# Expert sums added by a DMA from GpSimd's queue, a matrix inverse planned sooner, and ten stores moved to SyncE's queue

## The chip, the core and the metric

The kernel runs on one core of one Trainium2 chip. The metric is device time of one execution in microseconds (us); lower is better. The engines are named as in the profile: PE (TensorE, matmuls), PEld (its weight loads), DVE (VectorE), ACT (ScalarE), POOL (GpSimd), SP (SyncE, which here only issues DMAs). Each engine works through its own queue in order. DMAs are issued on the queues of SP, POOL and, at the start, ACT. A change of this kernel's time under about 0.2% (3 us) cannot be told from none.

## What is computed

A delta-rule attention feeds two expert layers:

```python
for t in range(S):                       # 768 steps, per batch (4) and head (8), D = 48
    y[:, :, t] = einsum('bhd,bhde->bhe', q[:, :, t], state)
    v_old = einsum('bhde,bhd->bhe', state, kt)
    state = state + bt * einsum('bhd,bhe->bhde', kt, vt - v_old)
x = y as (3072 tokens, 384)
for e in range(4):                       # experts: 384 -> 1024 -> 384
    out += p[:, e:e + 1] * (maximum(x @ w1[e], 0) @ w2[e])
gate = 1 / (1 + exp(-(out @ w_gate)));  return (gate * (out @ w_val)) @ w_out   # 384 -> 1536 -> 384
```

All is float32; each large matmul is done as three passes over split operands (high and low parts).

## The kernel before

**Tiling.** The sequence is cut into 12 steps of 64 positions; a step holds 256 tokens. Two steps make a pair of 512 tokens, and there are six pairs. For each pair PE runs four expert phases ("m1", 8 units each, `emit_a` and `emit_b`) and one gated phase ("m2", 12 units). In `emit_a` PE writes `ph` (line 759), ACT and DVE split it into `hhi` and `hlo`, and two units later `emit_b` sums into `acc` (line 796). A granule of weights comes in as `raw` (line 182, SP's queue, three buffers), and ACT and DVE split it into `ws`.

**Experts' sums.** At the end of an expert phase `finish` runs for the three row blocks d = 0, 1, 2. Expert 0 writes `ACC` directly. For the others DVE writes `ctmp`, the product of `acc` with the gate probabilities `pe`; then for experts 1 and 2 POOL adds it to `ACC` (line 837), and for expert 3 DVE adds it and ACT and DVE split the sum into `xhi` and `xlo` for m2. In the first pair the phases are cut differently: there two sets of three adds work on 256 columns.

**Attention.** Step c needs `XT`, the inverse of a triangular 64 x 64 matrix per head. `plan_g` makes `L` and `P` of a step (tile `LP`): the keys `KQ` are loaded on SP's queue, ACT copies them to `bdG` (lines 318 and 319), PE multiplies (`pg`, line 325), DVE scales. `l_out`, `l_off` and `p_out` then store them in DRAM (`ld`, lines 411 and 412; `pd`, line 428): five DMAs for a step from the fourth on. Once a pair is stored, `plan_inv` reads it back (`Lpp`), and DVE alone works out the inverse in 63 steps of two instructions each (`itmp`, then `Xpp`). `x_out` stores the result (`xd`, line 505, POOL's queue, two DMAs) and `x_in` reads it back in another layout (`XT`, line 508, POOL's queue). Then PE multiplies `pu` (line 357), and so on through the step's chain. `scale_v` (line 539) is two POOL multiplications of `V`, which DVE needs for `R`.

**Decode.** In the first 300 us the second layer's weights come in a packed form: ACT (`dec_scale`, lines 229 and 230), DVE and POOL (lines 239 and 240) unpack them, and POOL's queue stores them (`w_d`, line 252). They go round a few buffers, so a new ACT step waits until an older store has landed.

**Order.** The program is written out by a planner at build time. `plan(t, ...)` puts a task at a model time t of PE; `back` holds two lists, "dec" and "inv", of single DVE instructions with due times, and `fill` emits one when it is due and the model's DVE is at most 2.8 us ahead of PE. At `first` (14 or 8 us before a pair's chain) what is left of the inverse is emitted at once. `q[0]` is the queue on which stores and read-backs are issued; it is POOL's after the start.

Of the kernel before, what the change touches and what calls it, by code (L numbers as in the profile page):

```python
# [14 lines left out]
ALU = mybir.AluOpType  # L15
# [5 lines left out]
NE, FF1, FF2 = 4, 1024, 1536  # L21
# [20 lines left out]
CH1, CH2, TR1, TR2 = 78.0, 50.0, 44.0, 16.0  # L42
# [40 lines left out]
def moe_delta_kernel(  # L83
# [14 lines left out]
    nc = tc.nc  # L98
# [181 lines left out]
    q = [nc.sync, None, None]  # L280
# [109 lines left out]
    def l_out(c):  # L390
        lt = Lts[c % 2]
        r, c2 = INV_OF[c]
        steps, small = INV[r]
        l_done.add(c)
        lv = [lt[o : o + HC].rearrange("p i h t -> p (i h) t") for o in range(0, P, HC)]
        if small:
            if c2 == 0:
                ld_t[r] = dr.tile([len(steps), 2, 2, H, 2, HC, HC], F32, tag=f"ls{len(steps)}", name="ls")
                od_t[r] = dr.tile([len(steps), 2, H, 2, HC, HC], F32, tag=f"lo{len(steps)}", name="lo")
            for a in range(2):  # L400
                for bp in range(2):
                    q[0].dma_start(
                        out=ld_t[r][c2, a, :, :, bp].rearrange("i h s t -> s (i h) t"),
                        in_=lv[2 * bp + a][:, :, a * HC : (a + 1) * HC],
                    )
            return
        if c2 == 0:
            ld_t[r] = dr.tile([len(steps), 2, H, 2, HC, 3 * HC], F32, tag="ld", name="ld")
        for bp in range(2):
            ld = ld_t[r][c2, :, :, bp]  # L410
            q[0].dma_start(out=ld[:, :, :, 0:C].rearrange("i h s t -> s (i h) t"), in_=lv[2 * bp])  # L411
            q[0].dma_start(
                out=ld[:, :, :, C:].rearrange("i h s t -> s (i h) t"), in_=lv[2 * bp + 1][:, :, HC:]
            )

    def l_off(c):
        lt = Lts[c % 2]
        r, c2 = INV_OF[c]
        if INV[r][1]:
            for bp in range(2):  # L420
                q[0].dma_start(
                    out=od_t[r][c2, :, :, bp].rearrange("i h s t -> s (i h) t"),
                    in_=lt[bp * C : bp * C + HC].rearrange("p i h t -> p (i h) t")[:, :, HC:],
                )

    def p_out(c):
        pd_t[c] = dr.tile([P, 2 * H * C], F32, tag=f"pd{c % 2}", name="pd")
        q[0].dma_start(out=pd_t[c], in_=Pts[c % 2].rearrange("p i h t -> p (i h t)"))
# [375 lines left out]
    def finish(n, d):  # L804
        kind, b, e, s0, ns = PHASES[n]
        cols, w = slice(s0 * STEP, (s0 + ns) * STEP), ns * STEP
        if kind == "m2":
            o = (2 * b + s0) * STEP
            t = tp.tile([P, 2 * STEP], F32, tag="tmp", name="otmp")
            nc.scalar.copy(out=t[:, :w], in_=acc_t[d][:, :w])  # L810
            nc.sync.dma_start(out=out[d, :, o : o + w], in_=t[:, :w])
            return
        pe = p_t[n][:, :w]
        if e == NE - 1 and d == 0:
            x_hi[b, 2] = xp.tile([P, KT, 2 * STEP], F32R, tag="xhi", name="xhi")
            x_lo[b, 2] = xp.tile([P, KT, 2 * STEP], F32R, tag="xlo", name="xlo")
        new = [s for s in range(s0, s0 + ns) if (b, s, d) not in begun]
        begun.update((b, s, d) for s in new)
        for s in new:
            at = slice((s - s0) * STEP, (s - s0 + 1) * STEP)  # L820
            if len(new) == 2:
                at = slice(0, 2 * STEP)
            vec.tensor_tensor(
                out=ACC[:, d, cols][:, at], in0=acc_t[d][:, at], in1=pe[:, at], op=ALU.mult
            )
            if len(new) == 2:
                return
        if len(new) == ns:
            return
        if new:  # L830
            s1 = 1 - new[0]
            cols, w = slice(s1 * STEP, (s1 + 1) * STEP), STEP
            pe = pe[:, cols]
        a, ps = ACC[:, d, cols], acc_t[d][:, cols if new else slice(0, w)]
        t = gp.tile([P, 2 * STEP], F32, tag=("gv", "sg")[d % 2], name="ctmp")[:, :w]
        vec.tensor_tensor(out=t, in0=ps, in1=pe, op=ALU.mult)
        (nc.vector if e == NE - 1 else nc.gpsimd).tensor_tensor(out=a, in0=a, in1=t, op=ALU.add)  # L837
        if e == NE - 1:
            xh = x_hi[b, 2][:, d, cols]
            nc.scalar.copy(out=xh, in_=a)  # L840
            vec.tensor_tensor(
                out=x_lo[b, 2][:, d, cols], in0=a, in1=xh.bitcast(F32), op=ALU.subtract
            )
# [5 lines left out]
    W, M2 = {}, {}  # L849
# [8 lines left out]
    def plan(t, fn, kind=""):  # L858
        todo.append((t, len(todo), kind, fn))
# [86 lines left out]
    def plan_g(c, t):  # L946
        plan(t, lambda: load_kq(c))
        for i in range(2):
            plan(t + 12, lambda i=i: fill_bd(KQi, i))

        def g_task(i, hg):
            pg = g_bd(i, hg, KQi)
            g_l(pg, c, i, hg)
            g_p(pg, c, i, hg)

        for i in range(2):
            plan(t + 14 + 5 * i, lambda i=i: [g_task(i, hg) for hg in range(2)], "pe")
        plan(t + 23, lambda: (l_out(c), l_off(c), p_out(c)))

    class Turns:  # L960
        def __init__(self, *queues):
# [130 lines left out]
    with tc.manual_schedule():  # L1092
        pre_lo = xp.tile([P, KT, 2 * STEP], F32R, tag="xlo", name="pre_lo")
        dec_tiles()
        dpt, k2 = startup()
        q[1] = nc.sync
        vec_at[0] = 0.0
        plan(0.0, lambda: (gate_probs(dpt), load_p(0)))
        for i in range(2):
            plan(0.0, lambda i=i: s_task(0, i), "pe")  # L1100
        plan(0.0, lambda: load_ys(1))
        plan(11.0, lambda: nc.gpsimd.memset(bdG, 0.0))
        back["dec"].append((0.2, "dve", lambda: nc.scalar.square(out=k2, in_=k2)))
        back["dec"].append((1.0, "dve", lambda: norm_sum(k2, 2, 2)))
        back["dec"].append((1.5, "dve", lambda: norms(2, 4)))
        for c in (2, 3):
            back["dec"].append((2.0 + c, "dve", lambda c=c: (scale_l(c), l_out(c), l_off(c))))
        for c in (2, 3):
            back["dec"].append((4.0 + c, "dve", lambda c=c: (scale_p(c), p_out(c))))
        plan_chain(1, 1.0, 1.9)  # L1110
        plan_tr(1, 12.0, 1.0)
        plan_inv(1, *INV2)
        plan_decode(DEC0, DEC1)
        for k in range(1, NPAIR):
            w = W[k]
            if k > 1:
                r0 = max(M2[0] + 40.0, w - 270.0)
                plan_inv(k, r0, r0 + 22.0, w - CH1 - 14.0)
            if k + 1 < NPAIR:
                g0 = w - (161.0 if k > 1 else 116.0)  # L1120
                plan_norms(2 * k + 2, g0 - 8.0)
                plan_g(2 * k + 2, g0)
                plan_g(2 * k + 3, g0 + 26.0)
            plan_chain(2 * k, w - (CH1 if k > 1 else 84.0), 5.9)
            plan_chain(2 * k + 1, w - (CH2 if k > 1 else 46.0), 5.9)
            plan_tr(2 * k, w - (TR1 if k > 1 else 22.0), 4.0)
            plan_tr(2 * k + 1, w - (TR2 if k > 1 else 8.0), 4.0)
        todo.sort(key=lambda r: (r[0], r[1]))

        T, base = 0.0, 0  # L1130
        for n, (kind, b, e, s0, ns) in enumerate(PHASES):
            nf = NF1 if kind == "m1" else NF2
            part = unit_us(kind, ns) / (2 if kind == "m1" else 3)
            h = {}
            if kind == "m1":
                need = [(2 * b + s0 + s, i) for s in range(ns) for i in range(2)]
                while not all(q in x_done for q in need):
                    todo.pop(0)[3]()
            for u in range(nf):
                now[0] = T = T + part * (1 if kind == "m1" else 2)  # L1140
                h[u] = emit_a(n, base, u)
                slot()
                if u == 1 and n + 1 < len(PHASES):
                    load_p(n + 1)
                if LAG <= u < nf - 1:
                    now[0] = T = T + part
                    emit_b(n, base, [u - LAG], [h.pop(u - LAG)])
                    slot()
            now[0] = T = T + part * (LAG + 1)
            us = sorted(h)  # L1150
            emit_b(n, base, us, [h[u] for u in us])
            slot()
            base += NG1 if kind == "m1" else NG2
# [74 lines left out]
```

## Time and profile before

| | |
|---|---|
| median of 3 runs | 1490.71 us (1489.71 to 1491.36) |
| the profiled execution | 1488.77 us, of which 1487.1 us are its span |
| PE | 1430.0 us busy, 96% of the span |
| DVE | 1051.8 us, 71% |
| ACT | 585.0 us, 39% |
| POOL | 271.3 us, 18% |
| chain that ended last | PE 65%, by lines 759 (34%) and 796 (26%); DVE 2%, DMA 1% |

PE is busy nearly throughout. Read the 40 slices of 37 us first: they show where PE is not at nine tenths and where the granted clock falls. Then read PE's waits, each of which names the engine or the DMA that ended it, and the timeline around the longest of them. The clock of PE has two levels, 1.2 and 2.4 GHz; the profile gives it as a share of full speed.

### The profile page before, as it was taken

The page shows a single profiled execution, that of the slowest core. Times are in us where ns is not written, and L with a number is a line of the kernel's source. Part 1 is how long each engine was busy: PE and PEld are TensorE (multiplying, and loading weights), DVE is VectorE, ACT ScalarE, POOL GpSimd, SP SyncE. Part 2 cuts the span into 40 slices and gives each one's busy share as a digit, 9 for nine tenths or more (in the row PEclk, how much of TensorE's full clock was granted, in tenths as well). Part 3 has the DMA queues.
Part 4 walks back from the last instruction along what each step waited for, and adds up shares of the span by engine and source line. Part 5 has one row for each costly group of instructions (what it writes and reads, how often), then busy time and mean ns, then how long its engine had stood idle before and what let it go on. Part 6 is the DMA issues. An engine that isn't in the chain of part 4 may idle for free.

```text
span 1487.1 us, 24739 instructions
## 1 busy us (share of the span) xinstructions
PE 1430.0 (96%) x9703; PEld 1188.9 (80%) x9703; DVE 1051.8 (71%) x1805; ACT 585.0 (39%) x953; POOL 271.3 (18%) x318
## 2 busy tenths in 40 slices
PE   6899998999999799999999999999999999999999
PEld 5687876887877688888888888888888888888787
DVE  6579997847899577788667888667888655444553
ACT  4335554525433244343344343244433343333343
POOL 3165465710012200012200001310001210001000
PEclk7889999999999899999999999999999999999999
DMA  9485796695453855554684445585333553433231
GB/s 226 109 269 188 237 293 221 192 241 152 145 133 117 208 151 135 158 155 126 173 204 142 138 137 164 154 213 158 125 103 103 141 155 96 134 103 103 85 96 64
DMA packets 95668, 232.21 MB, mean 156 GB/s; under 512 B 24800, under 2 KB 28320, under 8 KB 93520
## 3 DMA queue, kind: packets, MB, share of 16 engines
q1 hardware_dynamic: 79760, 186.65, 42.5%
q0 software_dynamic: 11376, 42.54, 10.8%
q10 hardware_dynamic: 4416, 1.44, 0.4%
q8 instruction: 76, 1.25, 0.4%
q14 instruction: 40, 0.33, 0.1%
HBM read 199.74 MB, written 26.92 MB: 152 GB/s over the span
## 4 chain that ended last, share of the span: by engine, by line
PE 65%; DVE 2%; DMA 1%; issue 1%; ACT 0%; POOL 0%; DVEq 0%; ACTq 0%
PE ph L759 34%; PE acc L796 26%; PE pu L357 1%; PE pg L325 1%; PE pk L549 1%; PE yt L582 1%; PE ps L620 1%; PE yt L583 1%; DMA XT<-xd 0%; DMA xd<-Xpp 0%; DVE Xpp L110 0%; DVE itmp L110 0%; DVE ws L110 0%; DVE hlo L110 0%; DVE ctmp L110 0%
## 5 line engine op out<-in xcount | busy, mean ns | idle before, releaser
L759 PE MATMUL ph<-xhi,ws 128*128 128x512 f32 (+1 forms) x2064 | 632.2, 388 | 1.3 <-ACT xhi L840 0.8
L796 PE MATMUL acc<-hhi,ws 128*128 128x512 f32 (+1 forms) x1632 | 496.5, 386 | 1.9 <-ACT hhi L775 0.9
L759 PEld LDWEIGHTS ph<-xhi,ws 128*128 128x128 f32 x2064 | 381.8, 189 | 78.9 <-ACT xhi L840 1.2
L759 PE MATMUL ph<-xlo,ws 128*128 128x512 f32 (+1 forms) x1032 | 398.1, 386 | 0.3 <-DVE xlo L110 0.3
L796 PEld LDWEIGHTS acc<-hhi,ws 128*128 128x128 f32 x1632 | 304.5, 190 | 62.4 <-ACT hhi L766 1.6
L110 DVE TENSOR_TENSOR ws<-raw,ws 128x768 fp32r<-128x768 f32 x308 | 300.8, 980 | 46.1 <-ACT ws L190 42.8
L796 PE MATMUL acc<-hlo,ws 128*128 128x512 f32 (+1 forms) x816 | 315.1, 386 | 11.3 <-DVE hlo L110 11.3
L190 ACT CAST ws<-raw 128x768 fp32r<-128x768 f32 x308 | 252.6, 829 | 65.7 <-PE acc L796 60.1
L766 ACT ACTIVATE hhi<-ph 128x512 fp32r<-128x512 f32 (+1 forms) x200 | 116.2, 581 | 410.0 <-PE ph L759 407.1
L759 PEld LDWEIGHTS ph<-xlo,ws 128*128 128x128 f32 x1032 | 194.4, 188 | 41.0 <-DVE xlo L110 1.9
L110 DVE SCALAR_TENSOR_TENSOR hlo<-ph,hhi 128x512 fp32r<-128x512 f32 (+1 forms) x200 | 132.9, 666 | 116.7 <-ACT hhi L766 116.6
L796 PEld LDWEIGHTS acc<-hlo,ws 128*128 128x128 f32 x816 | 154.8, 190 | 44.8 <-DVE hlo L110 14.5
L110 DVE TENSOR_TENSOR itmp<-Xpp,Lpp 128x62 f32<-128x62 f32 (+29 forms) x344 | 165.8, 489 | 12.2 <-DMA Lpp<-ls 7.4
L110 DVE TENSOR_TENSOR Xpp<-Xpp,itmp 128x62 f32<-128x62 f32 (+29 forms) x344 | 165.3, 488 | 6.6
L110 DVE TENSOR_TENSOR gv<-ph,sg 128x512 f32<-128x512 f32 x72 | 49.7, 690 | 105.6 <-PE ph L759 92.7
L837 POOL TENSOR_TENSOR ACC<-ACC,ctmp 128x512 f32<-128x512 f32 (+1 forms) x39 | 50.9, 1313 | 345.1 <-DVE ctmp L110 344.7
L775 ACT CAST hhi<-gv 128x512 fp32r<-128x512 f32 x72 | 44.7, 621 | 160.6 <-DVE gv L110 160.6
L110 DVE TENSOR_TENSOR hlo<-gv,hhi 128x512 fp32r<-128x512 f32 x72 | 51.1, 710 | 49.4 <-ACT hhi L775 49.4
L411 POOL DMA_DIRECT2D ld<-LP x16 | 10.7, 670 | 352.8 <-DVE LP L110 352.8
L773 ACT ACTIVATE sg<-ph 128x512 f32<-128x512 f32 x72 | 43.0, 597 | 69.0 <-PE ph L759 68.9
L110 DVE TENSOR_TENSOR ctmp<-acc,pe 128x512 f32<-128x512 f32 (+1 forms) x57 | 37.5, 659 | 23.2 <-PE acc L796 23.1
L357 PEld LDWEIGHTS pu<-R,XT 64*64 64x64 f32 x1024 | 33.0, 140 | 14.5 <-issue 10.6
(169 smaller groups left out, 1042.5 us busy)
## 6 DMA issues: line engine op xcount, KB each, us to landing
raw<-in_wp SPq DMA_DIRECT2D x200, 384.0 KB, 3.1
raw<-w_d SPq DMA_DIRECT2D x108, 384.0 KB, 3.6
KQ<-in_kq SPq DMA_DIRECT2D x9, 896.0 KB, 7.5
Lpp<-ld POOLq DMA_DIRECT2D x8, 768.0 KB, 14.7
pe<-p_d SPq DMA_DIRECT2D x23, 256.0 KB, 4.2
dec_a<-in_wp SPq DMA_DIRECT2D x15, 384.0 KB, 5.2
Lpp<-in_wp SPq DMA_DIRECT2D x14, 384.0 KB, 4.6
pd<-LP POOLq DMA_DIRECT2D x10, 512.0 KB, 4.9
```

The source lines that it names most:

```text
L110: return fn(*args, **kw)
L190: nc.scalar.copy(out=w[:, 0], in_=t)
L325: nc.tensor.matmul(out=pg[:, j], lhsT=bdG[:, i, h], rhs=kq_t[i][0:112, :, h], start=True, stop=True)
L357: nc.tensor.matmul(out=out[o : o + C], lhsT=lhsT[o : o + C], rhs=rhs[o : o + C], start=True, stop=True)
L549: nc.tensor.matmul(out=pk[0:C, h], lhsT=KS[C:112, i, h], rhs=rhsA[C:112, i, h], start=True, stop=True)
L582: nc.tensor.matmul(out=dst[:, 0], lhsT=fa[:, cols], rhs=YQ[0:112, 0, i, h], start=True, stop=True)
L759: nc.tensor.matmul(out=res[q], lhsT=lt, rhs=rt, start=(k == 0 and j == 0), stop=(k == KT - 1 and j == 2))
L766: nc.scalar.activation(out=hh, in_=res[0], func=AF.Relu)
L773: nc.scalar.activation(out=sg, in_=res[0], func=AF.Sigmoid)
L775: nc.scalar.copy(out=hh, in_=gv)
L796: nc.tensor.matmul(out=acc_t[d][:, :w], lhsT=lt, rhs=rt, start=(u == 0 and j == 0), stop=(u == nf - 1 and j == 2),)
L837: (nc.vector if e == NE - 1 else nc.gpsimd).tensor_tensor(out=a, in0=a, in1=t, op=ALU.add)
```

## The change

Three things are edited. In `finish` the POOL addition for experts 1 and 2 becomes a DMA on POOL's queue that adds `ctmp` to `ACC` in SBUF (39 instructions in all). In `plan_g` the stores of `L` and `P` are put 1 us later and, for steps 4 and 5, issued on SP's queue (`l_off` has nothing to do for these steps and is no longer called). In the planner's loop the read of the inverse for pairs 2 to 5 is due 2 us sooner, its first DVE step 7 us sooner and its last 6 us sooner.

```diff
         vec.tensor_tensor(out=t, in0=ps, in1=pe, op=ALU.mult)
-        (nc.vector if e == NE - 1 else nc.gpsimd).tensor_tensor(out=a, in0=a, in1=t, op=ALU.add)
-        if e == NE - 1:
+        if e < NE - 1:
+            nc.gpsimd.dma_start(out=a, in_=t, accum_op=ALU.add)
+        else:
+            nc.vector.tensor_tensor(out=a, in0=a, in1=t, op=ALU.add)
             xh = x_hi[b, 2][:, d, cols]
...
-        plan(t + 23, lambda: (l_out(c), l_off(c), p_out(c)))
+        def leave():
+            q[0] = nc.sync if c < 6 else nc.gpsimd
+            l_out(c)
+            p_out(c)
+            q[0] = nc.gpsimd
+
+        plan(t + 24, leave)
...
-                r0 = max(M2[0] + 40.0, w - 270.0)
-                plan_inv(k, r0, r0 + 22.0, w - CH1 - 14.0)
+                r0 = max(M2[0] + 38.0, w - 270.0)
+                plan_inv(k, r0, r0 + 17.0, w - CH1 - 20.0)
```

PE's and ACT's queues keep their order. On DVE the steps of the inverses move against the rest. At the start of the inverse of steps 4 and 5 (`itmp 128x63` is its first instruction) DVE's queue changes like this, - before and + now:

```order
 L110 TENSOR_TENSOR hlo<-gv,hhi 128x512
 L110 TENSOR_TENSOR ws<-raw,ws 128x768
-L110 TENSOR_TENSOR gv<-ph,sg 128x512
-L110 TENSOR_TENSOR hlo<-gv,hhi 128x512
-L110 TENSOR_TENSOR ws<-raw,ws 128x768 x2
 L110 TENSOR_TENSOR itmp<-Xpp,Lpp 128x63
 L110 TENSOR_TENSOR Xpp<-Xpp,itmp 128x63
```

The first step now stands four instructions sooner; `gv`, `hlo` and `ws` follow a few steps later.

At the end of the same inverse (its last instruction is `Xpp<-Xpp,itmp 128x32`, three rows below these) the last splits of weights and hidden values ahead of it move down:

```order
 L110 TENSOR_TENSOR Xpp<-Xpp,itmp 128x30x4
 L110 TENSOR_TENSOR itmp<-Xpp,Lpp 128x93
+L110 TENSOR_TENSOR ws<-raw,ws 128x768
+L110 SCALAR_TENSOR_TENSOR hlo<-ph,hhi 128x512
 L110 TENSOR_TENSOR Xpp<-Xpp,itmp 128x31x3
 L110 TENSOR_TENSOR itmp<-Xpp,Lpp 128x62
```

The pair comes from above: before, it stood behind `itmp 128x252`, twelve instructions higher. What stands ahead of the inverse's last instruction, taken together, is the same as before.

On POOL's queue, in the decode, the five stores of step 4 go (those of step 5, thirty instructions later, go likewise):

```order
 L240 TENSOR_TENSOR Xpp<-Xpp,dec_a 128x384
 L252 DMA w_d<-dec_b 128x384
-L411 DMA ld<-LP_117 32x16x64
-L412 DMA ld<-LP_117 32x16x32
-L411 DMA ld<-LP_117 32x16x64
-L412 DMA ld<-LP_117 32x16x32
-L428 DMA pd<-LP_117 128x1024
 L539 TENSOR_TENSOR V<-V,nrm_all 128x384 x2
 L239 TENSOR_TENSOR dec_b<-dec_b 128x384
```

On SP's queue they now stand between a weight load and the load of `KQ` for the next step:

```order
 L225 DMA Lpp<-in_wp 128x768
 L182 DMA raw<-in_wp 128x768
+L411 DMA ld<-LP_117 32x16x64
+L412 DMA ld<-LP_117 32x16x32
+L411 DMA ld<-LP_117 32x16x64
+L412 DMA ld<-LP_117 32x16x32
+L428 DMA pd<-LP_117 128x1024
 L283 DMA KQ<-in_kq 112x2048
 L182 DMA raw<-in_wp 128x768
```

SP waits there for DVE to have written `LP`. Besides, on POOL's queue the two `xd` stores of the inverse of steps 4 and 5 now stand ahead of `scale_v`, where they stood behind it.

## Rows read from the trace of the kernel before

**Rows 1.** The page's part 2: PE's granted clock in 40 equal slices, in tenths.
```profile
PEclk7889999999999899999999999999999999999999
```
**Rows 2.** PE's waits: line waited for, us in total, times, longest.
```profile
PE acc L796 <- DVE hlo L110: 11.3, 7, 2.3
```
**Rows 3.** Timeline of PE: start, us, instruction, xcount, [idle before, what ended it].
```profile
243.21 1.01 PE L325 MATMUL pg<-KQ,bdG 112*128 112x128 f32 x3 [5.70 <-ACT bdG L319]
...
492.88 0.62 PE L796 MATMUL acc<-hhi,ws 128*128 128x512 f32 x2
...
506.65 0.41 PE L357 MATMUL pu<-R,XT 64*64 64x48 f32 x2 [7.49 <-DMA XT<-xd]
508.20 3.65 PE L357 MATMUL pu<-R,XT 64*64 64x48 f32 x62 [1.14 <-DMA XT<-xd]
```
**Rows 4.** Busy time by stretch: PE, PEld, DVE, ACT, POOL, clock, DMA share, GB/s.
```profile
240.00:260.00 20.00, 15.54 (x122) 13.21 (x123) 14.20 (x26) 10.06 (x18) 5.80 (x8) 0.83 0.54 174
342.30:481.20 138.90, 134.40 (x618) 110.29 (x617) 124.43 (x213) 52.90 (x82) 16.97 (x18) 1.00 0.48 138
500.00:520.00 20.00, 12.21 (x150) 10.55 (x151) 6.05 (x9) 3.90 (x7) 8.03 (x11) 0.74 1.00 225
```
**Rows 5.** The chain that ended last, in order of time: start, us, what.
```profile
517.72 7.70 PE ph L759 x33
...
733.15 6.12 PE acc L796 x27
...
747.10 7.71 PE ph L759 x33
```
**Rows 6.** Timeline of DVE.
```profile
346.21 0.22 DVE L110 TENSOR_TENSOR itmp<-Xpp,Lpp 128x63 f32<-128x63 f32 x1
...
464.68 0.58 DVE L110 TENSOR_TENSOR itmp<-Xpp,Lpp 128x408 f32<-128x408 f32 x1
465.29 1.55 DVE L110 TENSOR_TENSOR Xpp<-Xpp,itmp 128x408 f32<-128x408 f32 x1
...
481.17 0.68 DVE L110 SCALAR_TENSOR_TENSOR hlo<-ph,hhi 128x512 fp32r<-128x512 f32 x1
...
486.26 0.26 DVE L110 TENSOR_TENSOR Xpp<-Xpp,itmp 128x93 f32<-128x93 f32 x1
...
487.31 0.22 DVE L110 TENSOR_TENSOR Xpp<-Xpp,itmp 128x32 f32<-128x32 f32 x1
```
**Rows 7.** Timeline of ACT.
```profile
235.69 0.55 ACT L229 ACTIVATE Xpp<-dec_a 128x384 f32<-128x384 f32 x1 [5.06 <-DMA w_d<-Xpp]
...
478.62 0.60 ACT L766 ACTIVATE hhi<-ph 128x512 fp32r<-128x512 f32 x1 [2.76 <-PE ph L759]
```
**Rows 8.** Timeline of POOL in the decode.
```profile
223.71 0.69 POOL L411 DMA_DIRECT2D ld<-LP  x1
...
226.95 1.75 POOL L539 TENSOR_TENSOR V<-V,nrm_all 128x384 f32<-128x384 f32 x2
...
231.25 0.61 POOL L252 DMA_DIRECT2D w_d<-Xpp  x1
```
**Rows 9.** Timelines of DVE and of SP's queue around the stores of step 4.
```profile
216.75 0.41 DVE L110 TENSOR_TENSOR LP<-pg,mask_sb 128x256 f32<-128x256 f32 x1
...
215.69 0.40 SPq L283 DMA_DIRECT2D KQ<-in_kq  x1
220.82 0.33 SPq L182 DMA_DIRECT2D raw<-in_wp  x1
```
**Rows 10.** Busy time by stretch of 4 us in the decode, columns as above.
```profile
200.00:204.00 4.00, 2.80 (x19) 2.25 (x18) 3.90 (x7) 3.68 (x7) 3.08 (x3) 1.00 1.04 412
...
228.00:232.00 4.00, 4.00 (x20) 3.27 (x19) 3.96 (x7) 1.01 (x2) 3.90 (x5) 1.00 1.03 357
```
**Rows 11.** POOL's adds as a group (xcount, busy, mean ns, idle before), and a DMA group.
```profile
L837 POOL TENSOR_TENSOR ACC<-ACC,ctmp 128x512 f32<-128x512 f32 (+1 forms) x39 | 50.9, 1313 | 345.1 <-DVE ctmp L110 344.7
...
YQ<-pd POOLq DMA_DIRECT2D x20, 256.0 KB, 5.2
```

## The prediction

> **What bounds the kernel now.** PE is busy for 96% of the span, so only its idle time and its half-clock time can be won. I read the slices of the granted clock first [rows 1]: after the start-up the clock is at nine tenths or full except in one slice, the 14th (483 to 520 us). Then PE's waits [rows 2]: the waits for `hlo` come to 11.3 us in seven pieces, none over 2.3. Two others are longer, and the timeline of PE gives them [rows 3]: 5.70 us ending at 243.21, put down to ACT's `bdG`, and 7.49 + 1.14 = 8.63 us ending at 506.65 and 508.20, put down to the read-back of `XT`. The stretches around them show the third loss, the clock [rows 4]: it is 0.83 in 240 to 260 and 0.74 in 500 to 520, against 1.00 in 342 to 481. PE had stood idle just before each fall to the lower of its two levels. What the second place costs in all comes from the chain [rows 5]: from 492.88 [rows 3] to the 33 matmuls of `ph` at 517.72 are 24.84 us, while the same pass later, from the `acc` group at 733.15 to `ph` at 747.10, takes 13.95. The loss is 10.89 us, of which 8.63 are waiting and 2.26 the clock. For the first place: 20 us at 0.83 lack 3.4 us of clock; half of the 3.2 us in which PE still stood there cost nothing, which leaves 1.8. So the two places hold 5.7 + 1.8 + 8.6 + 2.3 = 18.4 us, and that is all I see that this change can reach.
>
> **The change, part by part.** *The inverse, sooner.* DVE ends the inverse of steps 4 and 5 at 487.31 + 0.22 = 487.53, and `XT` ends PE's wait at 506.65 [rows 3, 6]. Between stand only the issue of `xd` on POOL, two stores and two read-backs, so each us that DVE ends sooner is one less of the 8.63. DVE's queue is in order and the same work stands ahead of the last row as before; a start four instructions sooner than 346.21 [rows 6] alone gives nothing. What gives is idle time: DVE is busy 124.43 of the 138.90 us from 342.3 to 481.2 [rows 4], so 14.5 us are idle there, in which it stood at a matmul result or a weight load while inverse steps, which need neither, were queued behind. With the inverse steps due sooner these fill the gaps, and the splits come just in time. How far this goes is bounded by the last split that still stands ahead of the end: that `hlo` waits for ACT's `hhi`, which ends at 478.62 + 0.60 = 479.22 [rows 7]; then the `hlo` takes 0.68 and the rest of the inverse 1.27 (from 486.26 to 487.53) [rows 6]. So the end is 481.17 at the soonest, 6.4 us earlier. Of these 6.4, some 1.9 come from the POOL additions (below), and 4.5 must come out of the 14.5 idle us. I take the full 6.4, since less than a third of the idle time does it. The low end is 1.9, if no gap is filled. The rest of the wait at `XT` is then 8.6 - 6.4 = 2.2 us. Some `hlo` now stand behind a few inverse steps of 0.2 to 0.6 us [rows 6], which makes PE wait about 1 us before it comes to `XT`. That costs nothing as long as it stays below the rest of 2.2, which it shortens. With so short a rest I count the 2.3 us of clock as won; the other end is zero, since after a wait of up to 2.3 [rows 2] nothing here says which way the clock goes. `scale_v`, now behind `xd`, takes 1.75 us for its two instructions [rows 8]; what reads `V` stands ahead of the use of `XT`, which still comes some 19 us after the inverse. Sum: 6.4 + 2.3 = 8.7 us won. The later inverses move likewise, but in [rows 2, 3] no wait of PE hangs on them.
>
> *The stores on SP's queue.* POOL issues the five stores of step 4 from 223.71 until it goes on to `V` at 226.95 [rows 8], 3.24 us. Behind them stand the scaling of `V`, an unpacking step and, at 231.25, the store `w_d` from `Xpp`. ACT's next unpacking step writes into that buffer, begins at 235.69 and has waited 5.06 us for this store [rows 7]. ACT's copies to `bdG`, for which PE waits until 243.21, are queued behind. If POOL starts that store 3.2 us sooner, ACT goes on 3.2 us sooner and so does PE: 5.7 becomes 2.5. Of the 1.8 us of clock I take half, 0.9, since a rest is left; together 4.1. The bounds are zero, if the store lands no sooner for being issued sooner, and all of 5.7 + 1.8 = 7.5, if the path behind also gets shorter. On SP the five stores wait for `LP`, ready at 216.75 + 0.41 = 217.16. Queued behind them are the load of `KQ`, issued at 215.69 before, and a weight load at 220.82 [rows 9]. Five issues at 0.33 to 0.40 us end at about 219.2, so the weight load isn't late, and `KQ` goes out about 3.5 us later, long before the `bdG` that needs it (after 235). The cover of the weight load is 1.6 us; what exceeds it lands on the splits of weights. That the stores go out some 7 us earlier than 223.71 moves their bytes into another full stretch, but no more bytes.
>
> *The additions.* A POOL addition takes 1.31 us, 39 of them 50.9 us [rows 11]. POOL is not a bound, so their removal is worth only what it gives others: a DVE step of the inverse beside one takes 1.55 us where one of the same size takes 0.58 [rows 6]. That is 0.97 us, twice in the inverse of steps 4 and 5, and these 1.9 are in the sum above. What comes instead is a DMA of 256 KB (128 in the first pair) on POOL's queue, with an issue of about 0.6 us, like the DMA issues of [rows 8], so POOL is not later. The landing has no row. The nearest is `YQ<-pd`, also 256 KB on this queue, at 5.2 us [rows 11]; with two operands read I put it between that and 15. Its reader, the next `finish`, comes a phase later, and 30 phases in 1487 us make 50 us each. So outside the decode it is hidden: zero. In the decode the DMAs are full: the share is 1.04 in 200 to 204, just where three additions run (POOL 3.08, x3), and 1.03 in 228 to 232 [rows 10]. There the new bytes push others back. One set of 3 x 256 KB at 412 GB/s [rows 10] is 1.9 us, the two sets of 3 x 128 KB are 0.95 each, 3.8 in all if each byte is moved once and 11.4 if both operands are read and the sum is written. The loads that they push back are issued ahead of their use, and none of PE's two long waits of now is put down to one, so I take zero as the likeliest and 11.4 as the end.
>
> The sum is 8.7 + 4.1 = 12.8 us. The profiled execution took 1488.8, so 1476.0; the median of the runs lies 1.9 above it, which gives 1478.
>
> **Rivals.** *Only the inverse counts.* At 228 to 232 the DMA share is 1.03 [rows 10]: the store for which ACT waits would not land sooner, however soon POOL issues it, since the same bytes are ahead of it. Against it: POOL issues it at 231.25 and ACT starts 4.4 us later, less than the 5.2 of a 256-KB transfer, so no long queue stood ahead. Result: 8.7 alone, 1482. The Trainium skill, page "Trainium Kernel Development and Optimization", section "Key Constraints", speaks for this rival: DMAs from SP's, ACT's and POOL's queues share the same 16 DMA engines, and issuing from several saves only the sequencers' issue time. By that rule the move frees 3.24 us of POOL's issue time and no transfer time; the rows on the full DMA agree, and whether the issue time was on the path no run here has yet shown.
>
> *Only the stores count.* The gaps of DVE can lie where the queue isn't rearranged enough, for instance ahead of the first step; then DVE's end moves by the 1.9 of the additions or not at all. Result: 4.1, or 4.1 + 1.9, hence 1485 to 1486.5. Against it: the splits moved down at the end of the inverse by twelve instructions, which the change shows.
>
> *All goes.* Both waits vanish with their clock: 18.4 us, 1472. It needs the path after POOL's stores and the transfers of `xd` and `XT` to shorten too; the DMA share of 1.00 in 500 to 520 [rows 4] leaves little room.
>
> *Slower.* The accumulates crowd the full queues of the decode. Weight loads and unpacked stores come late, and PE waits for `ws`. The price is up to 11.4 us of transfer, and each of three such waits may take a fall of the clock with it, 1.8 us as at 243: 16.8. With nothing won by the stores and the 8.7 kept, that is 8.1 slower, 1499. It turns slower from about 11.7 us of added waits (8.7 and the 3 that can be told). For it speaks the share of 1.04 exactly at a set; against it, that three times the bytes and no slack at all are needed.
>
> **How the numbers follow.** A change under 0.2%, 3 us, can't be told from none. The forecast, 1478, gets 0.44; only the inverse, 1482, 0.22; only the stores, about 1485.7, 0.12; all goes, 1472, 0.10; slower, 1499, 0.07; nothing, 1490, 0.05. Faster by over 0.2%, below 1487.7: the first four, less 0.02 for the upper end of the stores alone: 0.86. Within 0.2%: 0.08, from "nothing" and that 0.02 and one of the slower case's 7 hundredths, where its price stays near the turning point. Slower: 0.06. For the range I leave out the slower case and nothing, 0.12. The rest reaches from 1472 to 1486.5; two more below, about the distance between the profiled execution and the median, and a half above make 1470 to 1487.
>
> **What would show it.** For the inverse: its last DVE step ending near 481, and PE's wait for `XT` of 2 to 3 us in place of 8.6, with the clock of 500 to 520 near 1.00. For the stores: the wait at `bdG` near 2.5 us, with POOL's store from `Xpp` near 228 and ACT's step behind it near 232.5. For the additions: no DVE step of the inverse beside a POOL operation at 1.5 us, and no wait of PE at the next `finish`. The forecast is wrong if the last step ends later than 485, if new PE waits for `ws` or `raw` stand in 140 to 240, or if longer `hlo` waits in 342 to 481 exceed 2.2 us.

## The result and the profile after

| | before | after |
|---|---|---|
| median of 4 runs each | 1490.78 us | 1477.64 us (1475.94 to 1477.94) |
| ratio, with 95% interval | | 0.9913 [0.9898, 0.9928] |
| profiled execution, of which span | 1488.77, 1487.1 us | 1475.94, 1474.2 us |
| PE busy | 1430.0 us, 96% | 1426.0 us, 97% |
| POOL busy | 271.3 us | 246.1 us |

The forecast was 1478, a gain of 12.8 us on the profiled execution. The two profiled executions differ by 12.8 us. The sum agrees. But inside it errors of both signs cancel, as the experiments show, and that is luck.

The page's slices of the granted clock and PE's waits for `hlo`, after (compare [rows 1, 2]):

```profile
PEclk7889999999999999999999999999999999999999
...
PE acc L796 <- DVE hlo L110: 9.1, 6, 2.4
```

The 8 of the 14th slice is gone. The timeline of PE at the places of [rows 3], with two rows ahead of `XT` (start, us, instruction, xcount, [idle before, what ended it]):

```profile
202.74 3.02 PE L325 MATMUL pg<-KQ,bdG 112*128 112x128 f32 x16 [3.55 <-issue]
...
241.64 2.05 PE L325 MATMUL pg<-KQ,bdG 112*128 112x128 f32 x16 [2.41 <-ACT bdG L319]
...
344.30 0.73 PE L796 MATMUL acc<-hhi,ws 128*128 128x512 f32 x2 [0.52 <-DVE ws L110]
348.29 0.73 PE L796 MATMUL acc<-hhi,ws 128*128 128x512 f32 x2 [1.66 <-ACT hhi L775]
...
496.29 2.07 PE L357 MATMUL pu<-R,XT 64*64 64x48 f32 x64
```

Where after has the two waits of 0.52 and 1.66 us, before had one:

```profile
350.22 0.73 PE L796 MATMUL acc<-hhi,ws 128*128 128x512 f32 x2 [0.95 <-ACT hhi L775]
```

At `bdG` 2.41 us are left of 5.70. At `XT` nothing is left of 8.63: the 64 `pu` matmuls run without a wait. The stretches of [rows 4] (us, PE, PEld, DVE, ACT, POOL busy, clock, DMA share, GB/s) show that the clock does not fall there in this execution:

```profile
240.00:260.00 20.00, 16.78 (x148) 13.98 (x150) 17.14 (x31) 9.77 (x16) 8.49 (x10) 1.00 0.65 195
...
500.00:520.00 20.00, 19.46 (x196) 16.02 (x195) 11.73 (x20) 10.84 (x17) 3.05 (x5) 1.00 1.00 230
```

The end of the inverse of steps 4 and 5 on DVE, with the `hhi` on ACT that the last `hlo` waits for (compare [rows 6, 7]):

```profile
475.81 0.60 ACT L766 ACTIVATE hhi<-ph 128x512 fp32r<-128x512 f32 x1 [2.76 <-PE ph L759]
```

```profile
476.44 0.69 DVE L110 SCALAR_TENSOR_TENSOR hlo<-ph,hhi 128x512 fp32r<-128x512 f32 x1
477.05 0.24 DVE L110 TENSOR_TENSOR Xpp<-Xpp,itmp 128x93 f32<-128x93 f32 x1
...
478.09 0.22 DVE L110 TENSOR_TENSOR Xpp<-Xpp,itmp 128x32 f32<-128x32 f32 x1
```

`hhi` ends at 476.41, `hlo` starts at 476.44, the inverse ends at 478.31. So the end stands at the bound that the prediction named.

Followed along ACT's instructions, which match one to one between the two traces, the gain builds up like this: 0 up to 199 us; minus 1.7 at 203 to 207, where PE waits 3.55 us in place of 1.20 and the clock falls behind the wait (before, it fell at 196); 3.3 from the wait at `bdG` and 2.0 from the clock behind it; minus 2.3 from longer waits between 344 and 430; 1.5 between 458 and 482; 10.9 at `XT`. That is 13.7, of which 0.2 go right behind `XT` and 0.6 at the very end, behind the last store. The loss at 203 can't be put down to the change: up to there the queues of no_stores (below) are the same as those of after, and in its profile PE doesn't wait there at all.

### The profile page after: what moved, and what is told of

It is laid out like the page before. It is cut to its first block, busy times and chain, and to the rows that moved or that the text cites. A ratio compares the mean times of both kernels' runs of the same rounds, so it can differ in the third digit from the quotient of the medians.

```text
span 1474.2 us, 24799 instructions
## 1 busy us (share of the span) xinstructions
PE 1426.0 (97%) x9703; PEld 1185.4 (80%) x9703; DVE 1038.3 (70%) x1805; ACT 585.3 (40%) x953; POOL 246.1 (17%) x308
## 4 chain that ended last, share of the span: by engine, by line
PE 83%; DVE 9%; issue 3%; DMA 3%; ACT 2%; POOL 0%; DVEq 0%; ACTq 0%; SPq 0%
PE ph L759 42%; PE acc L796 32%; PE pu L357 2%; DVE Xpp L110 2%; DVE itmp L110 2%; PE pg L325 2%; DVE ws L110 1%; DMA raw<-w_d 1%; PE pk L549 1%; DVE hlo L110 1%; PE ps L620 1%; PE yt L582 1%; PE yt L583 1%; DVE dec_b L110 0%; DMA KQ<-in_kq 0%
## 5 line engine op out<-in xcount | busy, mean ns | idle before, releaser
L110 DVE TENSOR_TENSOR itmp<-Xpp,Lpp 128x62 f32<-128x62 f32 (+29 forms) x344 | 160.6, 474 | 12.6 <-DMA Lpp<-ls 7.3
L110 DVE TENSOR_TENSOR Xpp<-Xpp,itmp 128x62 f32<-128x62 f32 (+29 forms) x344 | 159.7, 471 | 5.9
L838 POOL DMA_DIRECT2D ACC<-ctmp x39 | 35.0, 958 | 656.8 <-DVE ctmp L110 651.4
L110 DVE TENSOR_TENSOR ctmp<-acc,pe 128x512 f32<-128x512 f32 (+1 forms) x57 | 37.4, 659 | 20.7 <-PE acc L796 20.4
L325 PE MATMUL pg<-KQ,bdG 112*128 112x128 f32 x256 | 32.9, 283 | 8.1 <-issue 3.6
L325 PEld LDWEIGHTS pg<-KQ,bdG 112*128 112x128 f32 x256 | 31.4, 196 | 11.5 <-ACT bdG L319 5.2
```

Source lines behind the costliest of these rows:

```text
L110: return fn(*args, **kw)
L325: nc.tensor.matmul(out=pg[:, j], lhsT=bdG[:, i, h], rhs=kq_t[i][0:112, :, h], start=True, stop=True)
L838: nc.gpsimd.dma_start(out=a, in_=t, accum_op=ALU.add)
```

## Experiments

To see through the scatter of single executions, in which a fall of the clock more or less costs about 1.7 us, read the medians with their intervals first, and the profiles for where the time lies. In every table "end" is the time from the inverse's last DVE step to the moment PE is ready for `XT` (11.63 before, 18.05 after), and "transfer" the time from that step to the landing of the second `XT` (20.6 before, 17.6 after). The wait at `XT` is about the difference, where that is positive (the waits in the rows are 0.2 to 0.4 us shorter).

### One part alone

Additions alone:

```diff
-        (nc.vector if e == NE - 1 else nc.gpsimd).tensor_tensor(out=a, in0=a, in1=t, op=ALU.add)
-        if e == NE - 1:
+        if e < NE - 1:
+            nc.gpsimd.dma_start(out=a, in_=t, accum_op=ALU.add)
+        else:
+            nc.vector.tensor_tensor(out=a, in0=a, in1=t, op=ALU.add)
```

> Only the additions become accumulating DMAs. My theory: the inverse of steps 4 and 5 ends 1.9 us sooner (no step beside a POOL addition), the wait at XT shrinks by that, nothing else: 1488.9. Rival (accumulates crowd the DMA queues of the decode): new or longer waits of PE between 144 and 250, 1491 or more.

Stores alone:

```diff
-        plan(t + 23, lambda: (l_out(c), l_off(c), p_out(c)))
+        def leave():
+            q[0] = nc.sync if c < 6 else nc.gpsimd
+            l_out(c)
+            p_out(c)
+            q[0] = nc.gpsimd
+
+        plan(t + 24, leave)
```

> Only the stores of L and P of steps 4 and 5 go to SyncE's queue; additions and inverse as before. My theory: POOL's 3.2 us of issues stood on the path to bdG. The wait at bdG falls from 5.7 to about 2.4 us and the clock in 240 to 250 stays high; the waits at XT stay at 7.5 and 1.1. About 3.7 us faster, 1487. Rival (the DMAs share their engines, so the store behind lands no sooner): wait at bdG unchanged, 1490.8.

Dates of the inverse alone (the same kernel ran once more beside the later experiments, as only_inverse_b):

```diff
-                r0 = max(M2[0] + 40.0, w - 270.0)
-                plan_inv(k, r0, r0 + 22.0, w - CH1 - 14.0)
+                r0 = max(M2[0] + 38.0, w - 270.0)
+                plan_inv(k, r0, r0 + 17.0, w - CH1 - 20.0)
```

> Only the planner's dates of the inverse are changed. My theory: DVE ends the inverse of steps 4 and 5 some 4.5 us sooner against PE (6.4 with the additions gone from POOL), and the transfers of xd and XT take some 3 us less because fewer weight loads lie beside them; a wait of about 1 us at XT is left and the clock there stays high: about 9 us faster, 1482. The wait at bdG stays 5.7. If the transfers take as long as before, a wait of about 4 us and the fall of the clock are left: 1486. Rival (DVE is in order, the same work stands ahead): 1490.8.

> Only the dates of the inverse, on the same chip: tells what stores and additions are worth together once the wait at XT is gone. By the waits of the profiles: 5.8 against 2.4 us at bdG, 0.5 at XT, 1.1 at the hlo waits near 148: 4 to 5 us slower than after_b. By the rival (only the inverse counts): within 2 us of after_b.

| | median | ratio to before | wait at bdG | end | transfer | waits at XT |
|---|---|---|---|---|---|---|
| only_adds | 1489.51 | 0.9991 [0.9977, 1.0004] | 5.48 | 11.63 | 22.5 | 9.29 + 1.24 |
| only_stores | 1489.22 | 0.9991 [0.9978, 1.0004] | 3.48 | 11.63 | 20.7 | 7.58 + 1.13 |
| only_inverse | 1481.67 | 0.9938 [0.9919, 0.9956] | 5.79 | 17.05 | 17.8 | 0.51 |
| only_inverse_b | 1482.05 | 0.9946 [0.9932, 0.9961] | 5.62 | 17.03 | 19.6 | 2.27 |

The dates alone bring 8 to 9 us, as expected (with an end 5.4 us sooner where 4.5 were expected). The two others alone can't be told from no change. Look at the column "end": with the old dates it is 11.63 whatever else is changed. The additions, which I had put down for 1.9 us of it, moved it by nothing. The reason stands in the timelines of DVE and POOL with the additions alone:

```profile
460.88 0.58 DVE L110 TENSOR_TENSOR itmp<-Xpp,Lpp 128x408 f32<-128x408 f32 x1
461.49 2.73 DVE L110 TENSOR_TENSOR Xpp<-Xpp,itmp 128x408 f32<-128x408 f32 x1
```

```profile
461.26 0.86 POOL L838 DMA_DIRECT2D ACC<-ctmp  x1 [1.16 <-DVE ctmp L110]
461.83 1.94 POOL L539 TENSOR_TENSOR V<-V,nrm_all 128x384 f32<-128x384 f32 x2
```

The POOL addition beside this step is gone. But `scale_v` now starts a third of a us after the step and the step takes 2.73 us in place of 0.58, 2.15 more, until both multiplications are over. Before, the same stretch lost 0.97 to the addition at 465.29 [rows 6] and 1.02 to `scale_v` in the two rows behind it, which take 0.56 each where nothing runs beside them:

```profile
466.88 1.07 DVE L110 TENSOR_TENSOR itmp<-Xpp,Lpp 128x384 f32<-128x384 f32 x1
467.98 1.07 DVE L110 TENSOR_TENSOR Xpp<-Xpp,itmp 128x384 f32<-128x384 f32 x1
```

Together 1.99 against 2.15: nothing won. The other addition in this stretch also lengthened a step by 0.97, but what follows shows that DVE had idle time behind it. The Trainium skill, page "SBUF — State Buffer", section "Who interferes with whom", says that a DVE instruction with two inputs in SBUF contends with a GpSimd instruction that reads SBUF. These rows agree, and give the size: here the step was over only when POOL's two instructions were.

### Two parts, one undone

no_adds is the changed kernel with POOL's additions, no_stores with the stores back on POOL's queue, no_inverse with the old dates: the diffs above, each read the other way round.

> The changed kernel with POOL additions put back in place of the accumulating DMAs. My theory: the inverse ends 1.9 us later; the changed kernel's XT landed 0.4 us ahead of its use, so a wait of about 1.5 us comes back at XT: 1479. If the additions matter for nothing else, nothing else changes. Rival (the accumulates crowd the decode): faster than the changed kernel, under 1476.

> The changed kernel with the stores of L and P put back on POOL's queue, at their old place. My theory: the wait at bdG and the fall of the clock there come back: 3.7 us slower than the changed kernel, 1481.3. Rival (the additions' POOL time gave that place its gain): under 1478.5.

> The changed kernel with the old dates of the inverse. My theory: the XT wait comes back but for the 1.9 us of the additions, about 6.7 us in all, and its fall of the clock: 1490.8 - 3.7 - 1.9, about 1485. Rival (the additions or stores gave the XT gain): under 1480.

The median of no_stores is that of the changed kernel, so the two were run again on one chip:

> The changed kernel once more, on the same chip as the next three. 13 us faster than before, 1477.6. If the scatter between chips and runs hid a worth of the stores, this one is 2 to 3 us faster than no_stores_b.

> The changed kernel with the stores of L and P on POOL's queue at their old place, beside the changed kernel on one chip. My theory by the profiles: the wait at bdG is 4.6 us with them on POOL's queue and 2.4 on SyncE's, so 2.2 us slower than after_b, plus up to 1.7 where the clock falls longer. Rival (the medians so far): no difference.

| | median | ratio to before | wait at bdG | end | transfer | waits at XT |
|---|---|---|---|---|---|---|
| no_adds | 1478.65 | 0.9923 [0.9903, 0.9944] | 2.35 | 17.05 | 17.5 | 0.26 |
| no_stores | 1477.67 | 0.9914 [0.9900, 0.9928] | 4.59 | 18.05 | 18.6 | none over 0.3 |
| no_inverse | 1488.77 | 0.9987 [0.9976, 0.9998] | 3.64 | 11.63 | 22.5 | 9.00 + 1.49 |
| after_b | 1477.11 | 0.9916 [0.9901, 0.9931] | 3.00 | 18.05 | 17.2 | none |
| no_stores_b | 1478.88 | 0.9922 [0.9909, 0.9936] | 5.44 | 18.05 | 18.6 | 0.38 |

*The dates* decide: without them the gain is 0.1%, my 1485 for no_inverse was 4 us too fast. But they aren't all: only_inverse_b is 4.9 us slower than after_b on the same chip, as expected, so with the new dates the stores and the additions together are worth about that. *The additions* move the end by 1.0 us, from 17.05 to 18.05, in place of the 1.9 expected, and only with the new dates. With these, `scale_v` stands behind `xd`, after the inverse, and in no_adds two steps still run beside a POOL addition. These are the rows of DVE:

```profile
428.59 1.67 DVE L110 TENSOR_TENSOR itmp<-Xpp,Lpp 128x513 f32<-128x513 f32 x1
...
462.57 0.69 DVE L110 TENSOR_TENSOR ctmp<-acc,pe 128x512 f32<-128x512 f32 x1 [0.76 <-PE acc L796]
464.68 0.69 DVE L110 TENSOR_TENSOR ctmp<-acc,pe 128x512 f32<-128x512 f32 x1 [1.42 <-PE acc L796]
...
465.83 1.48 DVE L110 TENSOR_TENSOR Xpp<-Xpp,itmp 128x338 f32<-128x338 f32 x1
```

The first takes 0.70 us undisturbed, in before; DVE stands idle behind it, at `acc`, so its 0.97 us are made up. A step of the last one's size takes 0.50 us just before it, and behind it DVE has no idle time up to the end of the inverse. The additions have a second effect that I had not seen: a wait of PE in the first pair, next to the first set. In before and in after:

```profile
149.24 0.38 PE L796 MATMUL acc<-hlo,ws 128*128 128x256 f32 x1 [1.67 <-DVE hlo L110]
```

```profile
148.52 0.39 PE L796 MATMUL acc<-hlo,ws 128*128 128x256 f32 x1 [0.59 <-DVE hlo L110]
```

It is 0.59 to 0.64 in each of the profiles with the DMA, and 1.14 to 1.70 in all with POOL's additions.

*The stores*: the wait at `bdG` is 2.35 to 3.88 us in the seven profiles with the stores on SP's queue and ACT's order unchanged (3.15 on average), and 4.59 to 5.79 in the six with them on POOL's (5.44). That is 2.3 us, and the rival that the wait stays as it was falls. The medians show less than the forecast 4.1: 0.9 alone, 3.0 between only_inverse and no_adds, 0.0 and 1.8 between no_stores and the changed kernel, each uncertain by 2 to 3 us. The profiles show more: on PE's instructions, matched one to one, the place from 234 to 262 us of before gained 3.1 us on average in the seven and lost 0.2 in the six. Why the medians show less isn't settled.

### The price of accumulating

```diff
-            nc.gpsimd.dma_start(out=a, in_=t, accum_op=ALU.add)
+            nc.gpsimd.dma_start(out=a, in_=t)
```

> The changed kernel with each accumulating DMA replaced by a plain copy of the same size on the same queue (ACC gets the product in place of the sum, so the result leaves out the sums of the experts before). It prices the accumulating itself. My theory: it is hidden, 1477.6 and the same waits, landings of some 4 us a little shorter. Rival (both operands read, in the crowded decode): 2 us or more faster, with the waits at 199 to 204 and 239 shorter.

1477.12 us, ratio 0.9907 [0.9894, 0.9920]: as fast as the changed kernel. The groups of DMA issues (KB each, us to landing), of the changed kernel and of this one:

```profile
ACC<-ctmp POOLq DMA_DIRECT2D x33, 256.0 KB, 4.0
```

```profile
ACC<-ctmp POOLq DMA_DIRECT2D x33, 256.0 KB, 2.8
```

Accumulating costs 1.2 us of landing, and POOL 0.96 us an issue in place of 0.56. Both are hidden. (I had put the issue at 0.6 us and the landing at 5.2 or more.) In this profile PE waits 0.84 us at `XT`, with a transfer of 19.1 us. The forecast of "slower" by crowded queues falls with no_adds, since a plain copy moves bytes too: with POOL's additions back, the kernel isn't faster (1478.65).

### The copies to bdG sooner

```diff
-            plan(t + 12, lambda i=i: fill_bd(KQi, i))
+            plan(t + (8 if c < 6 else 12), lambda i=i: fill_bd(KQi, i))
```

> The changed kernel with ACT's copies to bdG for steps 4 and 5 four model us sooner, ahead of the unpacking steps that wait for stores (only ACT's order changes). My theory: the 2.4 us wait at bdG at 239 us is only a place in ACT's queue and goes, that of 3.6 us at 199 us shrinks too, with its 1.7 us fall of the clock; ACT's steps moved back by 2.5 us take some of it back: 1473 to 1475. Rival (what waits is the store, and the copies only push ACT's splits of weights later): same or slower, 1477.6 to 1480.

1479.08 us, 0.9917 [0.9904, 0.9929]: no gain, the time of the rival. PE's waits are these:

```profile
239.50 2.34 PE L325 MATMUL pg<-KQ,bdG 112*128 112x128 f32 x16 [2.21 <-ACT Y L562]
...
256.77 1.49 PE L325 MATMUL pg<-KQ,bdG 112*128 112x128 f32 x11 [2.54 <-DVE R L110]
```

At 237 PE waits 2.21 us, now put down to ACT's `Y`, and at 254 2.54 in place of 1.27 us: something there comes late in one order as in the other, but not the splits of weights that the rival names. The wait at 199 isn't in this profile; it is missing in five profiles of kernels without this edit too, so that isn't shown to be the edit's work.

### A later start of the inverse

```diff
-                plan_inv(k, r0, r0 + 17.0, w - CH1 - 20.0)
+                plan_inv(k, r0, r0 + 21.0, w - CH1 - 20.0)
```

> The changed kernel with the first step of the inverses due 4 model us later (its end keeps its date). In DVE's queue the last hlo ahead of the end of the inverse of steps 4 and 5 then stands 12 rows ahead of it, not 5. My theory: the inverse ends some 2.3 us later against PE; XT landed 0.4 us ahead of its use, so a wait of 1.5 to 2 us comes back at XT; the waits at 344 and 347 us (0.5 and 1.7) shrink to about 1.0 in all. Both together: within 1.5 us of after_b. Rival (XT has spare time): no wait at XT, 1 us faster.

1481.59 us, 0.9943 [0.9929, 0.9957]: 4.5 us slower than after_b beside it. The end is 13.92, 4.1 later than after's in place of the 2.3 expected, and the waits at `XT` are back. Of the waits at 344 and 347 one of 1.16 us is left, near the 1.0 expected. PE at `XT`:

```profile
500.23 0.42 PE L357 MATMUL pu<-R,XT 64*64 64x48 f32 x2 [4.70 <-DMA XT<-xd]
502.13 3.64 PE L357 MATMUL pu<-R,XT 64*64 64x48 f32 x62 [1.48 <-DMA XT<-xd]
```

2.2 of the 4.1 us are `scale_v`, which in this kernel stands ahead of `xd` again; it holds a step of the inverse:

```profile
461.58 2.72 DVE L110 TENSOR_TENSOR Xpp<-Xpp,itmp 128x375 f32<-128x375 f32 x1
```

The step before it in the same timeline, of the same size, takes 0.54. And the wait at `XT`, 6.2 us, is more than the 4.1: the transfers take 20.5 us in place of 17.6.

### Why the transfers get shorter

The groups of DMA issues from the first `xd` to the second `XT`, before and after:

```profile
xd<-Xpp POOLq DMA_DIRECT2D x2, 512.0 KB, 8.8
XT<-xd POOLq DMA_DIRECT2D x2, 256.0 KB, 7.0
KS<-in_kq SPq DMA_DIRECT2D x1, 448.0 KB, 8.3
V<-in_vt SPq DMA_DIRECT2D x1, 384.0 KB, 7.8
```

```profile
xd<-Xpp POOLq DMA_DIRECT2D x2, 512.0 KB, 7.7
Xpp<-in_xinit POOLq DMA_DIRECT2D x1, 1024.0 KB, 11.6
Lpp<-ld POOLq DMA_DIRECT2D x1, 768.0 KB, 15.3
XT<-xd POOLq DMA_DIRECT2D x2, 256.0 KB, 5.1
```

Before, the loads of `V` and `KS` for the next step were issued ahead of `XT`; after, `XT` is issued first and takes 5.1 us in place of 7.0, `xd` 7.7 in place of 8.8. Both loads stand ahead of `XT` in each of the five profiles with the end at 11.6 to 13.9 (issued 8.3 to 11.0 us after the inverse's last step, `XT` at 11.8 to 13.2) and behind it in each of the nine with the end at 17.0 to 18.1 (13.7 to 15.5, `XT` at 10.4 to 12.9). My reading is that SP's loads follow PE's progress, so that an inverse that ends sooner against PE slips in front of them. No run moves these loads alone: that they are what lengthens the transfers is argued, not shown, and one weight load more stands beside the transfers in the five as well. In the nine the transfer is 17.2 to 19.6 us, in the five 20.5 to 22.5. That it is 22.5 with the additions as DMAs and old dates, and 20.7 without, two profiles each, is not explained.

## Point by point

- *What bounds the kernel* held: nothing changed after 530 us but the 0.6 us behind the last store, and both places named paid.
- *The end of the inverse, 6.4 us sooner*: 18.05 - 11.63 = 6.42, to the bound by `hhi`. The way was partly another. I had 1.9 from the additions and 4.5 from idle time. The steps of the inverse got 3.1 us shorter in sum, 1.9 from the additions and 1.0 from `scale_v`, which the new dates moved out of the way. I had looked at `scale_v` only for who waits for `V`, and counted nothing for whom it holds up. From the same point of PE's work to the end of the inverse DVE was busy so long, before and after (columns of [rows 4]):

```profile
336.17:487.53 151.36, 146.86 (x672) 120.59 (x673) 133.66 (x235) 59.43 (x95) 16.97 (x18) 1.00 0.47 135
```

```profile
332.69:478.31 145.62, 140.41 (x643) 115.28 (x644) 129.71 (x235) 57.27 (x91) 11.68 (x16) 1.00 0.52 150
```

Its idle time shrank by 1.8 us only (17.7 to 15.9), its other work by 0.9, and 0.7 are no gain: PE itself lost them on this stretch and came later to `XT`. So the step "these 4.5 come out of the idle time" was mis-sized, and "1.9 from the additions" holds only where `scale_v` is away: 0 alone, 1.0 with the dates.
- *Each us of the end is one of the wait*: mis-sized. The transfers shrank too, by 3.0 us, so the whole 8.6 went, and the place gave 10.9 in place of 8.7. The 2.3 us of clock among them came with no wait left, where I had counted them as won with a wait of 2.2. In only_inverse_b 2.27 were left, and the clock fell behind them; in the other eight profiles with an end at 17.0 to 18.1 the wait was 0.84 or less, and it didn't. PE at `XT` in only_inverse_b, and the stretch:

```profile
502.86 2.06 PE L357 MATMUL pu<-R,XT 64*64 64x48 f32 x62 [2.27 <-DMA XT<-xd]
```

```profile
500.00:520.00 20.00, 17.71 (x213) 14.40 (x213) 10.46 (x16) 8.23 (x12) 5.15 (x6) 0.91 1.02 237
```

- *Later `hlo`, about 1 us, absorbed at XT*: failed as a step. The waits came at `ws` and at ACT's `hhi`, the price was 2.3 us between 344 and 430, and it was paid in full. The profile of after is the cheapest: on PE's matched instructions from 342 to 430 us of before, the nine profiles with an end at 17.0 to 18.1 lost 2.1 to 5.1 us, 3.5 on average, and in seven of them, not in after, the clock fell once or twice on the way. In after_b, the same kernel, it fell behind the wait at `hhi`:

```profile
340.00:362.00 22.00, 19.84 (x78) 15.26 (x78) 17.59 (x39) 9.79 (x16) 0.00 (x0) 0.92 0.59 177
```

The end of the inverse hangs on PE by `hhi`; where PE loses time, the end moves with it, and no rest at `XT` absorbs it.

- *The stores, 4.1*: the mechanism is there, the wait falls by 2.3 us on average (3.3 in the profile of after) and in five of the seven profiles with the stores on SP's queue the clock falls there less or not at all. The medians leave 0 to 3 us of it. In after itself POOL's store went out at 229.22, and ACT's step behind it began at 234.83 after 3.26 us of waiting, where I had 228 and 232.5. PE was 1.7 us behind before at this point, so against PE that is near what I had. The rule of the Trainium skill weighed ahead (page "Trainium Kernel Development and Optimization", section "Key Constraints"), that another issuing queue saves issue time only, agrees: the issue time was on the path, and the 2.3 us that the wait lost on average are no more than its 3.24.
- *The additions hidden*: right outside and inside the decode, as no_adds and the plain copy show. The 1.1 us at 149 was missed.

By parts the medians bear the forecast out: the dates alone bring 8.5 and 8.4 us where I had 8.7, the stores and additions on top of them 4.9 where I had 4.1, each uncertain by 2 to 3 us. That errors inside the parts cancel is luck. In the profile of after the place of `XT` paid 2.2 us more than forecast and that of `bdG` 5.3 in place of 4.1; the loss at 203 (1.7), the longer waits from 344 (2.3) and 0.8 behind `XT` took away more than that, and 1.5 between 458 and 482 came on top. None of the last four was in the sum.

## What to carry to other kernels

A chain that ends in DMAs can gain more than its own head start where the queues beside it are filled in step with the engine that waits: ask what it gets in front of. When an instruction on POOL changes place, look not only at who waits for its result but at which DVE steps it will now run beside. And a wait can only absorb losses ahead of it if what ends it doesn't depend on the engine that loses.

## What the runs showed of the hardware

A DVE step with two SBUF inputs beside two POOL multiplications took 2.73 us in place of 0.58, though by the trace it had begun 0.34 us ahead of them; beside a POOL addition, 1.55. An accumulating DMA of 256 KB from SBUF to SBUF landed in 4.0 us, a plain one in 2.8, and holds POOL for 0.96 and 0.56 us at the issue. Where the clock falls differs from execution to execution of the same queues: after and after_b are one kernel, and only in after_b did it fall between 330 and 440 us, for 1.7 us of lost time. At `bdG` it fell behind a wait of 2.35 us in no_adds and not behind one of 3.00 us in after_b.
